# The first two pairs of a fused scan-and-MLP kernel: other loads, another way to the products of a, another order

## The chip, the cores and the metric

The kernel runs on one core of one Trainium2 chip. The core has TensorE (PE, matrix products into PSUM; the profile shows its weight loads apart, as PEld), VectorE (DVE), ScalarE (ACT) and GpSimd (POOL), each with its own queue of instructions that it works off in order. SyncE (SP) issues most of the transfers, ACT a few; sixteen DMA engines carry them. The metric is the device time of one execution in microseconds, median of several runs.

## The reference

Four batches of eight heads, 768 tokens each. `x` has 32 values per token and head, `B` and `C` 16, `a` one decay between 0.85 and 0.95.

```python
log_a = np.log(np.clip(a, 1e-06, 1.0))
for c in range(nc):                      # chunks of the sequence
    cum = np.cumsum(la, axis=-1)
    L = np.exp(cum[..., :, None] - cum[..., None, :]) * causal
    CB = np.einsum('bhin,bhjn->bhij', Cc, Bc)
    y_intra = np.einsum('bhij,bhjd->bhid', CB * L, xc)
    y_inter = np.einsum('bhin,bhnd->bhid', Cc, state) * np.exp(cum)[..., None]
    y[:, :, sl] = y_intra + y_inter
    state = decay_full[..., None, None] * state + np.sum(Bx, axis=2)
# then, with y as tokens (3072 x 256):
h = x @ w_in                             # 256 x 2048
g = np.maximum(h, 0.0) + alpha * np.minimum(h, 0.0)
out = g @ w_out                          # 2048 x 256
```

The weights `w_in` and `w_out` arrive as 64-bit floats, all else as 32-bit.

## The kernel before

The sequence is cut into chunks of 128 tokens; two chunks are a pair, so there are twelve pairs, three to a batch. Two pairs make a group of 512 tokens. For each pair the kernel makes, for eight heads, the matrix of decays by running products (a scan on VectorE, with ones of the identity as restarts), the Gram products of C and B on TensorE, multiplies both, adds the state's part and writes the transposed tokens `xT`. Then the MLP of that group runs: hidden products, the two-sided slope (`s_alpha` on ACT, `s_mul` on VectorE), output products. Groups 1 to 5 use a scheme with seven products instead of eight; group 0 is done plainly.

The order of each engine's work is that of the program text: a manual schedule, with waits added where one instruction needs another. So an instruction that waits holds all behind it on its engine.

**Weights.** Sixteen pieces of 512 KB, of 256 columns of `w_in` or two blocks of `w_out`, are loaded in turn (`load_next`, L257) into six buffers and turned to 32-bit in parts: `convert_a` takes the size of the high word on ACT (L273), clamps it on GpSimd, or on VectorE for piece 0 (L278), and takes the low half on ACT (L283, L286); `convert_b` moves it into place on VectorE (L308) with the sign of L296; `convert` adds both parts on GpSimd (L330).

**The first two pairs** are written out in `first_two`. They work on half chunks of 64 tokens, so that their decays come from one scan a bank (L871). Their steps:

- Loads of `load_pair`: `a` of pair 0 and of pair 1, broadcast to the 16 rows of each head (`load_a`, L133), B and C by token with 64 B runs (L192), x with 128 B runs (L197), the row form of `a` (96 rows for two batches, L126), alpha (L207). For pair 0, C, the row form and alpha are issued by ACT, all else by SP. The loads of pair 1 follow two weight pieces and two small stores (L500, L477).
- `first_a` clamps `a` (L437) into `z0` and `z1`; `spread` (L865) lays a head's row over the tokens by matmul; `scan` makes the decays.
- The running products of `a` that the states need: for pair 0 a scan over the broadcast row (L1000), for pair 1 a scan over the row form (`rows_short`, L497), stored to DRAM as `short` and read back as a broadcast (`load_second`, L231).
- B and C are turned by TensorE against the identity and copied by ACT (`turned`, L843, L847); C is parted by even and odd heads on ACT (`spread_c`, L854).
- `bn` is B times the decays from each token (L533); `added` (L895) makes the state's increments, `states` (L906, L910) the states, `mask` (L916) their masked forms.
- `gram_of` (L881), `times` (L887), `x_products` (L929), `state_products` (L941), `copy_out` (L949).
- `keep_warm` (L338) issues products of ones that nobody reads.
- Alpha is turned (L992), copied (L994), and `slopes` makes the tables of it.
- `hidden_two` (L1110) makes hidden blocks f and f+1 of one half of group 0. Blocks 0 and 1 of the first half run between the two pairs. Of blocks 2 and 3 the eight matmuls are woven into pair 1's steps by the function `among`.
- For pair 2 on, `rows_clamp`, `rows_out` and `rows_products` store the clamped rows (`z`, L477) and the running products (`pf`, L447), which come back as broadcasts (`abc`, L160; `ap`, L168).

After `first_two` come `hidden_two` of the second half (L1110), then `hidden` (L1095) and `output` (L1142) of group 0, with pairs 2 and 3 between, and from about 78 us the seven-product scheme (L1241, L1216).

## Time and profile before

| what | value |
|---|---|
| runs, us | 355.75, 355.75, 356.41; median 355.75 |
| span of the profiled execution, us | 355.9 |
| busy, us and share of the span | PE 349.3 (98%), PEld 284.4 (80%), DVE 235.8 (66%), ACT 171.8 (48%), POOL 204.4 (57%) |
| moved by DMA | 30.24 MB in 105581 packets, 79896 of them under 512 B |
| share of the DMA engines, first twelve slices of 8.9 us, tenths | 7 8 9 9 9 8 9 6 0 7 3 4 |
| DMA of SP's queue, 0 to 60 us | 34030 packets, 13.51 MB, 87.7% of 16 engines |

The profile was taken of one execution, and its times are of that execution alone. A row of a timeline reads: start, length, engine, line, operation, what is written and read, count, and in brackets the idle time of the engine before it and what ended that. A row of the chain of waits reads: start, length, engine and line; it follows back from the last instruction what each step waited for. SPq and ACTq rows are issues of transfers. A wait that came from several engines is put down to one of them. A busy TensorE is not one at its peak, as matmuls overlap.

### The profile page before, as it was taken

The page shows a single profiled execution, that of the slowest core. Times are in us where ns is not written, and L with a number is a line of the kernel's source. Part 1 is how long each engine was busy: PE and PEld are TensorE (multiplying, and loading weights), DVE is VectorE, ACT ScalarE, POOL GpSimd, SP SyncE. Part 2 cuts the span into 40 slices and gives each one's busy share as a digit, 9 for nine tenths or more (in the row PEclk, how much of TensorE's full clock was granted, in tenths as well). Part 3 has the DMA queues.
Part 4 walks back from the last instruction along what each step waited for, and adds up shares of the span by engine and source line. Part 5 has one row for each costly group of instructions (what it writes and reads, how often), then busy time and mean ns, then how long its engine had stood idle before and what let it go on. Part 6 is the DMA issues. An engine that isn't in the chain of part 4 may idle for free.

```text
span 355.9 us, 7778 instructions
## 1 busy us (share of the span) xinstructions
PE 349.3 (98%) x2985; PEld 284.4 (80%) x2985; DVE 235.8 (66%) x482; ACT 171.8 (48%) x391; POOL 204.4 (57%) x228
## 2 busy tenths in 40 slices
PE   8899999999999999999999999999999999999996
PEld 4576665578788888888888888888888888888885
DVE  6876986998748756847747856757856633643363
ACT  3477576535355346345345445345445344443431
POOL 6776568589939855725646626637526535434520
PEclk9999999999999999999999999999999999999999
DMA  7899989607345403503423423422001001001102
GB/s 138 182 202 270 329 174 279 148 17 159 106 83 128 102 3 75 104 2 77 78 57 74 86 51 71 85 55 65 11 2 31 0 2 29 2 1 31 31 0 59
DMA packets 105581, 30.24 MB, mean 85 GB/s; under 512 B 79896, under 2 KB 101448, under 8 KB 105544
## 3 DMA queue, kind: packets, MB, share of 16 engines
q1 hardware_dynamic: 103048, 29.43, 36.3%
q10 hardware_dynamic: 2496, 0.32, 0.6%
q8 instruction: 23, 0.38, 0.5%
q14 instruction: 14, 0.11, 0.1%
HBM read 26.32 MB, written 3.42 MB: 84 GB/s over the span
## 4 chain that ended last, share of the span: by engine, by line
PE 89%; SPq 4%; DMA 3%; DVE 2%; ACT 1%; POOL 1%; issue 0%; DVEq 0%; ACTq 0%
PE bank L1216 33%; PE hp L1241 29%; PE bank L1142 6%; PE ss L1241 6%; PE hp L1095 3%; DMA raw<-in_moe_w_in_dram 2%; SPq L192 2%; PE ss L787 1%; PE ss L731 1%; PE hp L1110 1%; PE bank L1209 1%; PE ss L805 1%; PE ss L779 1%; DMA xt<-in_x_dram 1%; SPq L197 1%; PE ss L742 1%
## 5 line engine op out<-in xcount | busy, mean ns | idle before, releaser
L1298 POOL TENSOR_TENSOR gt<-gt 128x512 f32<-128x512 f32 x58 | 74.2, 1279 | 21.1 <-DVE gt L1226 16.3
L1216 PE MATMUL bank<-gt,w_out 128*128 128x256 f32 x320 | 83.5, 381 | 0.0
L1216 PEld LDWEIGHTS bank<-gt,w_out 128*128 128x128 f32 x320 | 60.1, 190 | 9.2 <-issue 1.0
L1288 POOL TENSOR_TENSOR gt<-gt 128x512 f32<-128x512 f32 x20 | 25.4, 1269 | 62.5 <-DVE gt L1226 49.7
L1226 DVE SCALAR_TENSOR_TENSOR gt<-hp,s_mul,gt 128x256 f32<-128x256 f32 x96 | 42.0, 479 | 29.1 <-ACT gt L1224 26.8
L1224 ACT ACTIVATE gt<-hp,s_alpha 128x256 f32<-128x256 f32 x96 | 40.3, 471 | 34.5 <-PE hp L1241 31.4
L1216 PE MATMUL bank<-gt,ws 128*128 128x256 f32 x224 | 55.9, 379 | 0.0
L1216 PEld LDWEIGHTS bank<-gt,ws 128*128 128x128 f32 x224 | 42.3, 190 | 5.6
L1241 PE MATMUL hp<-xs,w_in 128*128 128x256 f32 x160 | 41.9, 384 | 0.0
L1241 PE MATMUL hp<-xs,ws 128*128 128x256 f32 x160 | 41.1, 380 | 0.0
L1267 DVE TENSOR_TENSOR hp<-hp,u 128x512 f32<-128x512 f32 x20 | 14.0, 700 | 35.2 <-ACT u L1265 35.2
L1241 PEld LDWEIGHTS hp<-xs,ws 128*128 128x128 f32 x160 | 30.3, 190 | 4.3 <-POOL xs L1183 0.2
L1241 PEld LDWEIGHTS hp<-xs,w_in 128*128 128x128 f32 x160 | 29.7, 190 | 4.5
L1142 PE MATMUL bank<-w_out,gt 128*128 128x256 f32 x128 | 31.1, 385 | 0.4 <-POOL w_out L330 0.4
L1142 PEld LDWEIGHTS bank<-w_out,gt 128*128 128x128 f32 x128 | 23.6, 190 | 7.2 <-issue 2.9
L1241 PE MATMUL ss<-xT,w_in 128*128 128x256 f32 x96 | 24.6, 379 | 0.0
L645 POOL TENSOR_TENSOR sm<-state,bmask 128x256 f32<-128x256 f32 (+1 forms) x10 | 6.2, 620 | 29.0 <-DVE state L642 29.0
L1095 PE MATMUL hp<-xT,w_in 128*128 128x512 f32 x48 | 22.8, 596 | 0.0
L561 DVE TENSOR_TENSOR_SCAN dec<-abc,bank 128x192 f32<-128x192 f32 x48 | 22.7, 522 | 0.0
L1256 ACT COPY m<-hp 128x512 f32<-128x512 f32 x8 | 4.7, 586 | 35.7 <-PE hp L1241 35.7
L1265 ACT COPY u<-hp 128x512 f32<-128x512 f32 x20 | 11.7, 585 | 19.4 <-PE hp L1241 19.4
L1226 DVE SCALAR_TENSOR_TENSOR gt<-c,s_mul,gt 128x256 f32<-128x256 f32 x40 | 20.6, 555 | 0.0
(232 smaller groups left out, 608.2 us busy)
## 6 DMA issues: line engine op xcount, KB each, us to landing
abc<-z SPq DMA_DIRECT2D x24, 192.0 KB
raw<-in_moe_w_in_dram SPq DMA_DIRECT2D x8, 512.0 KB
raw<-in_moe_w_out_dram SPq DMA_DIRECT2D x8, 512.0 KB
abc<-z SPq DMA_DIRECT2D x8, 512.0 KB
out_dram<-o_sb SPq DMA_DIRECT2D x32, 64.0 KB
nat<-in_B_dram SPq DMA_DIRECT2D x26, 64.0 KB
xt<-in_x_dram SPq DMA_DIRECT2D x12, 128.0 KB
xt<-in_x_dram SPq DMA_DIRECT2D x24, 64.0 KB
```

Of the source, the lines that this page charges most:

```text
L192: eng.dma_start(out=nat[:, i, k].rearrange("p (h n) -> p h n", h=H), in_=src[b, :, ts, :].rearrange("h p n -> p h n"))
L561: nc.vector.tensor_tensor_scan(out=dv[:, o : o + SQ], data0=abc[k][:, s : s + SQ], data1=ident_p[0][:, :SQ], initial=0.0, op0=ALU.mult, op ...
L1095: nc.tensor.matmul(hp, w_in[:, k, f * P : (f + 1) * P], xts[g][:, k], start=(k == 0), stop=(k == KC - 1))
L1142: nc.tensor.matmul(pos[0][t // 2][:, t % 2], gt[:, t * Q : (t + 1) * Q], w_out[:, f], start=(f == 0 and t % 2 == 0), stop=(f == NF - 1), s ...
L1216: nc.tensor.matmul(ms[g][i][:, h], w, blocks[g, z][n][:, p], start=(q == 0 and h == 0), stop=(q == NQ - 1), skip_group_check=True)
L1224: nc.scalar.mul(o[:, p], h[:, p], s_alpha[:, fs[p]])
L1226: nc.vector.scalar_tensor_tensor(out=o[:, p], in0=h[:, p], scalar=s_mul[:, fs[p]], in1=o[:, p], op0=ALU.mult, op1=ALU.max)
L1241: nc.tensor.matmul(to[:, p], w(2 * z + p), b, start=start and p == 0, stop=True, skip_group_check=True)
L1265: nc.scalar.copy(out=u2, in_=A)
L1267: nc.vector.tensor_tensor(out=Y, in0=Y, in1=u2, op=ALU.add)
L1288: nc.gpsimd.tensor_tensor(out=tc_, in0=g22, in1=g12, op=ALU.subtract)
L1298: eng.tensor_tensor(out=o, in0=x0, in1=x1, op=ALU.subtract)
```

## The change

The diff touches the loads of pairs 0 and 1, `first_two`, and small parts that these use.

- **a.** Pair 0's `a` is read with another stride, one run of 1 KB for each of 128 partitions, of which one per head holds the head's row. Pair 1's has one partition per head (8 runs), in a tile that VectorE clears first.
- **Products of a.** `short` is neither stored nor read back, and the scan of pair 0 goes. Both pairs' products come from the row form: a table `heads` of ones picks the row of each head by matmul (`products`), and ACT copies the results.
- **C.** C of both pairs comes in runs of 512 B (`load_blocks`, as pairs 5 on have it), and VectorE turns it (`turn_c`) straight into its place. B alone is turned by TensorE.
- **Order of loads.** SP: a, C, a of pair 1, x, weight piece 0, alpha, all of pair 1, piece 1. ACT: rows, B of pair 0. The stores of `z` and `pf` stand behind pair 1's work.
- **Engines and order.** Clamping pair 1's `a` goes to GpSimd. Piece 0 is converted by halves (`convert_first`), with the copies of pair 0's result in the middle. Piece 1's clamp goes to VectorE, and its conversion stands behind the scans of pair 1. Blocks 2 and 3 of the first half follow pair 1's products in one piece. Some of the `keep_warm` products get shorter, one goes, two come.

```diff
-    WARM = 2
-    def load_a(t, b, c, eng=nc.sync):
-        first = a[b, 0:1, c * Q : (c + 2) * Q]
-        eng.dma_start(out=t, in_=bass.AP(tensor=first.tensor, offset=first.offset,
-                                             ap=[[S, H], [0, N], [1, 2 * Q]]))
+    def load_a(t, c, spread=False):
+        first = a[0, 0:1, c * Q : (c + 2) * Q]
+        if spread:
+            nc.sync.dma_start(out=t, in_=bass.AP(tensor=first.tensor, offset=first.offset,
+                                                 ap=[[S // N, P], [1, 2 * Q]]))
+        else:
+            nc.sync.dma_start(out=t.rearrange("(h n) t -> h n t", n=N)[:, 0],
+                              in_=a[0, :, c * Q : (c + 2) * Q])
+    def load_blocks(nat, i, src, b, c):
+        for e in range(2):
+            first = src[b, e : e + 1, c * Q : (c + 2) * Q, :]
+            nc.sync.dma_start(out=nat[:, 1 + e, i],
+                              in_=bass.AP(tensor=first.tensor, offset=first.offset,
+                                          ap=[[2 * S * N, P // 32], [8 * N, 32], [1, 8 * N]]))
+    def turn_c(nat, to):
+        nc.vector.transpose(to.rearrange("p (c b) -> p b c", b=8),
+                            nat[:, 1:3, 1].rearrange("p e (b n) -> p b e n", n=N))
...
         def load_bc(k):
-            for i, src in enumerate((B,) if turned else (B, C)):
-                eng = nc.scalar if gp == 0 and i else nc.sync
+            eng = nc.scalar if gp == 0 else nc.sync
+            if gp == 0 and k == 0:
+                load_blocks(nat, 1, C, b, c)
+            for i, src in enumerate((B,) if turned or gp < NB else (B, C)):
...
+            if gp == 1 and k:
+                load_blocks(nat, 1, C, b, c)
...
+            if gp == 0 and k:
+                load_a(loads["a", 1], 2)
...
+    def convert_first(dst, src, sg, copies):
...
+        magnitude(0)
+        low(0)
+        magnitude(1)
+        nc.vector.tensor_single_scalar(out=r, in_=hi, scalar=SIGN, op=ALU.bitwise_and)
+        for k in range(2):
...
+        copies()
+        low(1)
+        for k in range(2):
+            nc.gpsimd.tensor_tensor(out=d[:, k], in0=r[:, k], in1=g.bitcast(U32)[:, k], op=ALU.add)
...
-    keep_warm(ps_h.tile([P, GT], F32, name="hp"), WARM, GT)
+    first = ps_h.tile([P, GT], F32, name="hp")
+    keep_warm(first, 1, GT)
+    keep_warm(first, 1, Q)
...
         if i == 0:
             scratch["z", 0] = dr.tile([RW, Q], F32, name="z0")
-            nc.sync.dma_start(out=scratch["z", 0], in_=held.pop("z"))
+            nc.gpsimd.memset(held[0][:, :1], 0.0)
+            nc.sync.dma_start(out=scratch["z", 0], in_=held[0][:, :Q])
...
+        def products(rpf, i, to):
+            for k in range(2):
+                nc.tensor.matmul(to[:, k * Q : (k + 1) * Q], heads[:, 2 * i + k], rpf,
+                                 start=True, stop=True, skip_group_check=True)
...
+        spread(z0, sp)
+        clamp(nc.vector, rq[:, :Q], rows)
+        clamp(nc.gpsimd, starts_r[:RW, ::HQ], rows[:, ::HQ])
+        masks_halved()
+        z1 = first_a(loads["a", 1], nc.gpsimd, lent[1][:, 2:])
+        heads = prep.tile([RW, 4, P], F32, name="heads")
...
+        turn_c(nat0, ct0)
+        prq, rpf = rows_short(rq)
         for r in range(4):
             scan(0, r, sp[r])
...
+        turn_b(nat0, hp)
+        copy_b(bc0, hp[:, : 2 * Q])
         bn0 = pair_loads(0)
+        for i in range(2):
+            products(rpf, i, pfs[:, 2 * i * Q : 2 * (i + 1) * Q])
+        nc.scalar.copy(out=pf0, in_=pfs[:, : 2 * Q])
+        cd0 = decayed_c(bc0, pf0)
+        nc.tensor.transpose(misc[:, Q : Q + NF], al_n, ident[:NF, :NF])
+        nc.scalar.copy(out=alpha, in_=misc[:, Q : Q + NF])
         gram_of(bc0, cz0, sp)
...
-        keep_warm(sp[0], 1, GT)
+        keep_warm(sp[0], 1, Q)
+        spread(z1, sp)
...
+        convert_first(*pieces[0], lambda: copy_out(0, y))
+        convert_next(first=False, ready=moe_w_in.dtype != F32)
+        keep_warm(sp[0][:, 2 * Q :], 1)
+        turn_c(nat1, ct1)
+        for r in range(4):
             scan(1, r, sp[r])
...
+        prelu_of = {0: hidden_two(0, 0, 0, first)}
         bn1 = pair_loads(1)
...
         added(dps, bn1, xt1)
+        gram_of(bc1, cz1, sp)
+        keep_warm(own[1][:, : 2 * Q], 2)
         states(1, dps, pf1, range(3))
         one_at_a_time(1, range(3))
+        convert_a(*pieces[1], by=nc.vector)
+        prelu_of[0](False)
+        convert_b(*pieces[1])
+        convert_next(first=False)
+        for r in range(4):
+            times(1, r, sp[r])
+        states(1, dps, pf1, (3,))
+        y = places([own[0], bank(0)], [bank(1), bank(2)])
+        x_products(y, xt1, 1)
+        state_products(y, 1, cd1)
+        copy_out(1, y)
+        prelu_of[0]()
+        prelu_of[2] = hidden_two(0, 2, 0, second)
+        rows_clamp(0)
         rpf = rows_products()
         load_bc()
         load_next()
+        rows_out(0)
         rows_sent(rpf)
...
-    load_next(2)
+    load_next()
+    nc.sync.dma_start(out=al_n, in_=moe_alpha.rearrange("(k p) -> k p", p=P))
+    load_pair(1)
+    load_next()
```

## The prediction

> **What bounds the kernel now.** I read the share of each engine first, then TensorE's busy time by stretches, its waits, the chain of waits of the first 48 us, and last the single instructions of each queue there. The stretches (columns: stretch, its length, then busy time and count of PE, PEld, DVE, ACT, POOL; PEclk, DMA share, GB/s):
>
> ```profile
> 0.00:5.00 5.00, 4.17 (x21) 1.66 (x29) 2.97 (x13) 1.28 (x1) 3.66 (x16) 1.00 0.64 85
> ...
> 10.00:15.00 5.00, 4.15 (x106) 2.64 (x86) 4.60 (x14) 3.01 (x8) 2.84 (x5) 1.00 0.83 144
> 15.00:20.00 5.00, 4.75 (x83) 3.49 (x81) 3.44 (x7) 2.60 (x7) 4.80 (x8) 1.00 1.01 210
> ```
> ```profile
> 46.00:100.00 54.00, 54.00 (x432) 39.20 (x433) 43.83 (x75) 28.10 (x58) 41.03 (x41) 1.00 0.58 146
> 100.00:200.00 100.00, 100.00 (x823) 85.82 (x822) 67.11 (x136) 50.24 (x120) 58.76 (x61) 1.00 0.35 71
> ```
>
> From 46 us on TensorE never stops. Whatever the change does must show as an earlier or later start of that unbroken row; behind 46 us it edits nothing. Before 46 us, the only waits of TensorE from 18 us on are these:
>
> ```profile
> PE bank L1142 <- POOL w_out L330: 0.4, 1, 0.4
> PE bank L929 <- DVE dec L887: 0.3, 1, 0.3
> ```
>
> So from about 24 us TensorE runs dense, with one hole of 0.44 us at 45.4. The end is set by two runners: the front (pairs 0 and 1, done at about 24 us) and the weights that land behind it. The chain shows both:
>
> ```profile
> 14.22 3.28 DMA xt<-in_x_dram
> ...
> 23.28 2.35 PE hp L1110 x10
> 25.63 1.74 PE bank L1110 x8
> ...
> 29.84 7.45 DMA raw<-in_moe_w_in_dram
> ...
> 44.52 1.28 POOL w_out L330
> 45.84 1.99 PE bank L1142 x8
> ```
>
> The front waits until 17.5 for x of pair 1; the weight piece that lands at 37.3 leads, through conversions, to the hole.
>
> **The loads.** Prices: the B and C loads of 64 B runs moved 1126 packets in 0.50 us (23.75 to 24.25), so 1024 take 0.46 us; x at 128 B moved 1426 in 1.00 us, so a tile takes 0.72; weights at 2 KB moved 186 in 1.00 us, so a piece of 256 takes 1.4. C in 512 B runs has no row. Its bounds are 64 KB at the 364 GB/s of the weights, 0.18 us, and 0.46 (no gain); I take 0.22, nearer the larger runs. Four C blocks save 1.0 us. The a row of pair 1 shrinks from 128 packets to 8 and the broadcast of `short` goes: 128 KB each at 364 GB/s, 0.35 each. The store of `short` saves about 0.1. In all 1.8 us of transfer less (bounds 0.8 to 1.9), and SP no longer sits in issues like this one:
>
> ```profile
> 9.40 3.52 SPq L192 DMA_DIRECT2D nat<-in_B_dram  x1
> ```
>
> New order on SP: a, C, C, a of pair 1, x, x, weights 0, alpha, then B, B, C, C, x, x of pair 1, weights 1. Pair 1 passes weights 1 and two stores; the alpha row leaves ACT's queue for SP's, behind 512 KB. B of pair 0 moves to ACT's queue. Packets of pair 0 (96 rows of 512 B, 128 of 1 KB, 2048 of 64 B, 256 of 512 B, 2048 of 128 B) cost, by the prices above, about 3.3 us of full rate against 4.1 before. Before, they were through at about 7.0; so 6.2 after. Weights 0 then end at 7.6, alpha just behind. A transfer is usable later than its last packet: the alpha row's queue ran dry at 5.4, and its reader started at 6.66, 1.2 us later. So **alpha lands at 8.8**. Bounds: 7.4 (straight after x, if the small row overtakes), and 10.3, since weights 0 before were read at 11.54 though by rate they ended at 8.9, a lag of 2.65. I take the small row's own lag. Pair 1's x ends 0.9 + 0.4 + 1.4 after 7.6 and lands at 11.5, six us earlier than 17.5, and is no gate any more.
>
> **The alpha wait.** Alpha's transpose stands ahead of the Gram products on TensorE, and alpha's copy ahead of the first state on ACT. These rows show the steps of before:
>
> ```profile
> 6.66 0.14 PEld L992 LDWEIGHTS ss<-ident,al_n 16*128 16x128 f32 x1 [0.17 <-DMA al_n<-in_moe_alpha_dram]
> 8.27 0.73 PE L881 MATMUL bank<-cz,bc 32*64 32x128 f32 x32 [0.53 <-ACT alpha L994]
> 8.97 0.76 DVE L887 TENSOR_TENSOR dec<-bank,dec 128x256 f32<-128x256 f32 x2 [0.40 <-PE bank L881]
> ```
>
> Gram began at 8.27, VectorE's products 0.70 later. Now Gram begins 0.2 after alpha, at 9.0, and the products at 9.7. Without alpha the gate would be VectorE's scans: first scan 5.55 before; its queue gains a transpose of C (0.55, half of the 1.11 that line 574 takes for twice the elements) and par (0.17), loses memsets, and may start about 0.2 earlier, as the warming matmuls no longer hold the spread until 4.5. Scans end at 8.4 against 7.98. So alpha costs 1.3 us there; SP's loads behind it are not held, as SP does not wait.
>
> **VectorE from there.** Its steps before x products of pair 1, from their rows: products and states of pair 0, 8.97 to 11.34, 2.37; weights 0, sign 0.40, clamp 0.43, xor 0.76, 1.59; transpose of C, 0.55; four scans, 2.43; three states, 0.92; weights 1, sign, clamp (now VectorE's, was GpSimd's) and xor by start-to-start steps, 0.34 + 0.34 + 0.61 = 1.29; four products, 1.36. Sum 10.5; end at 20.2. Before they ended at 21.50: **1.3 us earlier**. The removed scan for the products of a (0.67) and the clamp of a (0.28, now GpSimd's) are already out of this sum; rows_products (0.83) and its GpSimd clamp (0.63) move behind it. The head products, four small matmuls, lie in TensorE's idle time before Gram; if that cover went they would cost about 0.4, four times the 0.1 step of a transpose.
>
> One stall can come in: weights 0 end in ACT's second low half, behind copy-out, then a GpSimd half (0.85), then bn of pair 1 (1.15), which TensorE needs for the states. Worked through, it delays states by 0 to 0.65; I take 0.1, since before bn1 ended at 16.89, which is where VectorE's scans end now (16.6).
>
> **What it gives back on TensorE.** Before, hidden 2 and 3 of the first half were woven among pair 1's products: when these ended at 23.28, two of eight matmuls remained, and the second half began near 23.9. Now all eight follow. Eight at 0.217 (25.63 to 27.37 for eight) are 1.74 against 0.61: **1.1 us lost**. Copy-out hides beneath it. So the dense row begins 1.3 - 0.1 - 1.1 = 0.1 earlier.
>
> **The hole.** GpSimd's clamp of rows, rows_products, z's store and pf's store now follow pair 1 on their queues: z is stored near 22.4 (it was 7.38), pf near 22.9 (24.15). SP stands there: x of pair 2, weights 5, the decay broadcasts and weights 6 wait behind. Weights 2 to 4 are issued ahead and land meanwhile. Before, weights 6 were issued at 29.84; now pf + 2 us to land, broadcast, 0.5 each for four issues: about 26. With 1.8 us less to move, weights 6 land 2 to 3 us before 37.3, and the 0.44 closes. If this cover failed, an earlier front would only lengthen the hole.
>
> Later small gains: VectorE gets weights earlier, and TensorE's steps of 1.81 and 1.83 instead of 1.72 around 31 to 35 may shrink: 0.2 (0 to 0.4). **Sum**: 0.1 + 0.44 + 0.2, about 0.8 us off. The span is 355.9; the median of the runs, 355.75, lies 0.15 below it. 355.75 - 0.8 = **354.9**.
>
> The Trainium skill, TensorE: Matmul & The Clock Gate, Part 1, speaks against the change: an array that has been idle for about 3.4 us runs at half clock until as long a busy stretch has passed. This trace bears on it: four matmuls of 512 columns take 3.75 us at the start, 0.94 each, and 1.72 at 25 us and later, 0.43 each, while the granted clock reads 1.00 in both. By the rule, warming cut to about 2.3 us might leave the array slow beyond 9 us; the sum would then be some 1.5 us longer. I leave it out of the forecast.
>
> **The rivals.**
> *Larger gain.* Alpha lands by 7.5, so scans gate at 8.4, and VectorE's row begins 1.1 us earlier: 353.8, with up to 0.6 more where start-to-start steps are shorter than I took: 353.3. For it: the row is 8 KB. Against: it stands behind 512 KB on each ring.
> *Slower by alpha.* Each us that alpha lands after 8.8 is one us on Gram, VectorE and the end. It breaks even at 9.6 and costs 0.2% from 10.3. With the 2.65 lag of weights 0 it lands at 10.3; with the full bn stall, 0.55 more, 354.9 + 1.5 + 0.55 = 357.0. For it: the row of 11.54. Against: those weights had 512 KB more behind them, now small packets follow.
> *Slower by the clock.* Half speed for Gram (0.73 more) and for the hidden matmuls after the waiting stretch of 18 to 20 us (up to 1.7): 354.9 + 1.5 = 356.4. For it: the trimmed warming; against: a burst of matmuls ahead of that stretch.
> *The weights pin it.* If weights 6 come no earlier, the hole swallows the front's gain: 355.75. Against: all rows above.
> *Not what it says:* C in 512 B runs saves nothing: 1.0 us of transfer back, which lands on alpha by half: 355.3.
>
> **How the numbers follow.** Forecast (353.9 to 355.7 as its own range) 0.44; larger gain 0.26; alpha late 0.13; clock 0.07; weights pin it, and no saving, 0.10. A run of this kernel can be told from no change by about 0.2%, that is outside 355.04 to 356.46. The forecast's 0.44 splits into 0.28 faster, 0.12 same and 0.04 slower, the clock's 0.07 into 0.02 same and 0.05 slower, the last 0.10 into 0.08 same and 0.02 slower. Faster: 0.28 + 0.26 = 0.54. Same: 0.12 + 0.02 + 0.08 = 0.22. Slower: 0.13 + 0.04 + 0.05 + 0.02 = 0.24. The range runs from the larger gain to the alpha case, 353.0 to 357.0.
>
> **What would show it.** Right: alpha's transpose on TensorE waits for its DMA until about 8.8, VectorE's products of pair 0 start near 9.7, those of pair 1 end near 20.2, x of pair 1 is waited for by nobody, the second half of hidden begins near 23.8, and no wait for weights stands at 45 us. Wrong: a Gram stage begun by 8.3; matmuls of 256 columns at 0.43 instead of 0.217 after 9 us; a TensorE wait for a weight piece between 24 and 46 us; scans of pair 1 after 17.5.

## The result, and the profile after

| | runs, us | median, us | profiled execution, span us |
|---|---|---|---|
| before | 355.75 355.75 356.41 356.80 356.20 | 356.20 | 355.9 |
| changed | 365.19 366.95 367.18 367.05 367.40 | 367.05 | 363.5 |

The changed kernel is slower: the ratio is 1.0297, with a 95% interval of 1.0274 to 1.0321. The forecast of 354.9 us with a range of 353.0 to 357.0 was wrong in size and in sign.

The stretches of the changed kernel show first that TensorE runs short of work (columns as before; the second number is PE busy, the number behind POOL's is the granted clock):

```profile
0.00:5.00 5.00, 3.63 (x36) 1.97 (x36) 1.94 (x11) 1.90 (x2) 2.93 (x14) 1.00 0.58 99
5.00:10.00 5.00, 2.71 (x11) 2.48 (x12) 3.70 (x8) 1.53 (x4) 1.70 (x2) 1.00 0.89 184
10.00:15.00 5.00, 4.71 (x134) 3.32 (x133) 2.92 (x10) 1.92 (x7) 2.72 (x7) 1.00 0.96 261
15.00:20.00 5.00, 4.50 (x67) 3.06 (x73) 4.28 (x8) 3.22 (x10) 2.66 (x6) 1.00 0.80 154
20.00:25.00 5.00, 2.15 (x72) 1.43 (x73) 3.17 (x9) 0.92 (x3) 2.28 (x5) 1.00 0.67 161
25.00:30.00 5.00, 4.99 (x84) 4.16 (x85) 2.53 (x8) 1.72 (x6) 2.14 (x4) 0.54 0.16 36
30.00:35.00 5.00, 5.00 (x20) 4.21 (x19) 2.88 (x7) 3.00 (x8) 3.84 (x6) 0.77 1.03 307
```

TensorE has two holes, at 5 to 10 us and at 20 to 25 us. Behind the second the granted clock falls to 0.54, and from 25 to 35 us TensorE is busy throughout and still slow. The 1.00 of the first rows is no measurement: the trace's list of granted clocks begins at 11.79 us, with the rise to full speed. The two longest waits of TensorE name both holes:

```profile
PE ss L970 <- DVE dec L928: 2.8, 1, 2.8
PE ss L1035 <- DVE gt L538: 2.1, 1, 2.1
```

VectorE's queue shows where its time went (L152 is the new transpose of C, L538 the scan of the row form, L928 the products of decays and Gram matrices, L912 the scans of pair 1, L951 the states, L385 a warming product):

```profile
5.78 0.64 DVE L152 STREAM_TRANSPOSE bc<-nat 128x256 f32<-128x256 f32 x1 [2.02 <-DMA nat<-in_C_dram]
6.48 0.42 DVE L538 TENSOR_TENSOR_SCAN gt<-rq,gt 96x128 f32<-96x128 f32 x1
...
11.95 0.76 DVE L928 TENSOR_TENSOR dec<-bank,dec 128x256 f32<-128x256 f32 x2 [2.40 <-PE bank L922]
...
17.69 2.43 DVE L912 TENSOR_TENSOR_SCAN dec<-bank,ident_q 128x256 f32<-128x256 f32 x4 [0.68 <-PE bank L385]
...
22.16 0.60 DVE L951 SCALAR_TENSOR_TENSOR gt<-gt,ap,ss 128x64 f32<-128x64 f32 x2 [1.40 <-PE ss L385]
...
24.50 1.41 DVE L928 TENSOR_TENSOR dec<-bank,dec 128x256 f32<-128x256 f32 x4
```

It idles 2.02 us for C, and the row scans, which had nothing to do with C, stand behind that wait. It idles 2.40 us for the Gram products, and twice (0.68 and 1.40) for a product that nobody reads. TensorE ahead of the Gram products (L896 are the head products, L1047 is alpha, L922 Gram, L936 the increments):

```profile
8.72 1.91 PE L896 MATMUL ss<-gt,heads 96*128 96x128 f32 x8
10.57 0.28 PE L1047 MATMUL ss<-ident,al_n 16*128 16x16 f32 x1
10.78 1.16 PE L922 MATMUL bank<-cz,bc 32*64 32x128 f32 x32
11.87 0.59 PE L936 MATMUL hp<-xt,bn 64*32 64x64 f32 x32
```

Alpha waited for nothing. The four head products are eight records and take 1.91 us, where the forecast had idle time, or 0.4. Up to the Gram products TensorE runs at half speed; the increments are the first at full speed. The chain of waits tells the rest of the story, from pair 1's warming to the end of the second half's hidden products:

```profile
21.06 1.08 PE ss L385 x4
22.16 0.29 DVE gt L951
22.48 0.28 DVE gt L951
22.76 0.50 DVE wr L343
23.26 0.61 DVE wt L325
23.93 0.57 issue
24.50 0.43 DVE dec L928
24.97 0.24 PE ss L970
...
28.52 5.52 PE hp L1154 x16
34.04 1.73 PE bank L1154 x8
```

While VectorE makes the states and converts weight piece 1 (L343, L325, and L355 inside the gap that reads "issue"), TensorE has nothing from 22.13 to 24.97. Then sixteen records of hidden products take 5.52 us, 0.345 each, where the eight behind them take 1.73, 0.216 each.

By milestones, from the timelines of both kernels. Two rows of before that the table needs, the last scans and the decay products of pair 1:

```profile
16.31 1.26 DVE L871 TENSOR_TENSOR_SCAN dec<-bank,ident_q 128x256 f32<-128x256 f32 x2
...
20.08 1.42 DVE L887 TENSOR_TENSOR dec<-bank,dec 128x256 f32<-128x256 f32 x4
```


| stretch | before, us | changed, us | difference |
|---|---|---|---|
| start to pair 0's first decay product | 8.97 | 11.95 | +2.98 |
| from there to the end of pair 1's scans | 8.60 | 8.17 | -0.43 |
| to the end of pair 1's decay products | 3.93 | 5.79 | +1.86 |
| to the end of its state products | 1.78 | 2.61 | +0.83 |
| to the end of the second half's hidden products of 256 columns | 4.09 | 7.25 | +3.16 |
| sum | 27.37 | 35.77 | +8.40 |

Behind that TensorE is dense in both, and the changed kernel has no wait for weights left. So +8.40 less the hole of 0.44 and some small gains gives the 7.6 between the two spans. The runs differ by 10.85. In every run of the study that lists both, the time is the span plus about 1.7 us; by that the profiled execution of before took 357.6, longer than any of the five listed, and that of the changed kernel, 365.19, is the shortest of its five. So the table sets a long execution beside a short one and leaves some 3.2 us out. A likely part of these is seen in e1, e2, e3 and e10 below: with the changed kernel's warming they first reach full speed at 19.0 to 23.0 us, where the profile shown here does at 11.8. The changed kernel's longer runs were not profiled, so this is not shown.

### The profile page after: what moved, and what is told of

It is laid out like the page before. It is cut to its first block, busy times and chain, and to the rows that moved or that the text cites. A ratio compares the mean times of both kernels' runs of the same rounds, so it can differ in the third digit from the quotient of the medians.

```text
span 363.5 us, 7792 instructions
## 1 busy us (share of the span) xinstructions
PE 352.7 (97%) x2989; PEld 289.5 (80%) x2989; DVE 238.8 (66%) x484; ACT 173.0 (48%) x394; POOL 202.9 (56%) x226
## 4 chain that ended last, share of the span: by engine, by line
PE 95%; DVE 2%; DMA 1%; issue 0%; SPq 0%; POOL 0%; ACT 0%; DVEq 0%; POOLq 0%
PE bank L1256 33%; PE hp L1281 28%; PE bank L1182 8%; PE hp L1139 6%; PE ss L1281 6%; PE hp L1154 2%; PE ss L830 1%; PE ss L774 1%; DMA nat<-in_C_dram 1%; PE bank L1249 1%; PE ss L848 1%; PE ss L822 1%; PE ss L785 1%; PE ss L661 1%; PE ss L385 1%; PE bank L922 0%
## 5 line engine op out<-in xcount | busy, mean ns | idle before, releaser
L1281 PEld LDWEIGHTS hp<-xs,w_in 128*128 128x128 f32 x160 | 29.7, 190 | 4.5
```

The lines of the kernel that those rows point to most:

```text
L1281: nc.tensor.matmul(to[:, p], w(2 * z + p), b, start=start and p == 0, stop=True, skip_group_check=True)
```

## The experiments

The line numbers in an experiment's rows are those of its own kernel and can differ by one to four from the changed kernel's. Ratios are against the kernel before.

**e1: a filled hole.** Warming products in the gap ahead of pair 1's x products.

```diff
         states(1, dps, pf1, (3,))
+        keep_warm(second, 3, GT)
         y = places([own[0], bank(0)], [bank(1), bank(2)])
```

> The changed kernel with three more warming products of 512 columns on TensorE, written to a bank nobody reads, in its idle stretch of 22.1 to 25.0 us. Clock theory (the idle stretch halves TensorE's clock from 25.3 to 32.2 us): granted clock 1.00 all through, x products of pair 1 to the end of hidden 0 to 3 in 8.1 us instead of 10.8, total 2.5 to 3.5 us less (about 363.5 against 367). Rival (the clock is a bystander, VectorE and the weights set the pace behind 25 us): clock 1.00 and total within 0.7 us of 367.

365.49 us (362.58 to 366.09), ratio 1.0223 (1.0175 to 1.0271). The timeline of VectorE:

```profile
19.59 2.44 DVE L912 TENSOR_TENSOR_SCAN dec<-bank,ident_q 128x256 f32<-128x256 f32 x4 [1.82 <-PE bank L385]
...
25.46 0.60 DVE L951 SCALAR_TENSOR_TENSOR gt<-gt,ap,ss 128x64 f32<-128x64 f32 x2 [1.40 <-PE ss L385]
```

The clock is held: the granted clock reads 1.00 from 20 to 50 us. But only some 1.6 us come back. In the profiled execution the warming waits ahead of pair 1 were longer (1.82 instead of 0.68), and the profile has a wait for weights again (0.26). The longer waits are not the edit's doing: up to there the program is that of the changed kernel, but this execution stayed at half speed up to 23.0 us. The first hidden products, first in the changed kernel's profile, then in e1's:

```profile
17.81 2.17 PE L1154 MATMUL hp<-xT,w_in 128*128 128x256 f32 x8
```
```profile
19.77 3.51 PE L1155 MATMUL hp<-xT,w_in 128*128 128x256 f32 x8
```

So the late clock loss is a consequence of the gap, and not all of the loss; and half speed in the front lasts longer in some executions of one program than in others.

**e2: rows first.** The row scans ahead of the transpose of C on VectorE, the copy of the row products ahead of C's parting on ScalarE.

```diff
-        turn_c(nat0, ct0)
         prq, rpf = rows_short(rq)
+        turn_c(nat0, ct0)
```

> The changed kernel with the two scans of the row form ahead of the transpose of C on VectorE, and the copy of the turned row products ahead of the first spread of C on ACT. Theory that the wait for C (VectorE idle to 5.78 us) holds the front through the queue order: the row scans end near 5 instead of 7.2, the head products begin before 8, the first products of pair 0 on VectorE begin near 10.5 instead of 11.95, total 1.2 to 2 us less. Rival (the Gram stage is held by the head products at half clock or by C itself): they begin after 11.5, total within 0.6 us.

366.37 us (365.48 to 367.25), ratio 1.0274 (1.0249 to 1.0299). Alpha's transpose on TensorE:

```profile
9.15 0.28 PE L1047 MATMUL ss<-ident,al_n 16*128 16x16 f32 x1 [0.74 <-DMA al_n<-in_moe_alpha_dram]
```

With C's wait out of the row scans' way, alpha becomes the gate that the forecast named, at 9.15 instead of 8.8. Pair 0's decay products start at 10.53 instead of 11.95, 1.4 us earlier. Pair 1's scans then wait 1.82 us for the warming product in their bank, in an execution that reaches full speed only at 19.0 us. So the start moved as expected and the time did not: the median is 0.7 us less, and the interval overlaps that of the changed kernel.

**e3: warming elsewhere.** The warming behind pair 1's Gram products goes to a bank that nobody waits for.

```diff
-        keep_warm(own[1][:, : 2 * Q], 2)
+        keep_warm(second[:, 2 * Q :], 2)
```

> The changed kernel with the two warming products after the Gram stage of pair 1 written to the bank of the turned B instead of the bank that holds the states' increments. Bank theory (VectorE's second and third state wait for these products): VectorE's states end near 21.4 instead of 22.8, its products of pair 1 end near 24.5 instead of 25.9, TensorE's idle stretch shrinks to about 1.4 us, the clock stays at 1.00, total 4 to 5 us less. If the stretch alone does not set the clock: 1.4 us less and the clock drops as before. Rival (the states wait for the increments themselves): nothing moves.

364.83 us (364.37 to 365.47), ratio 1.0232 (1.0214 to 1.0251). The 1.40 is gone: VectorE makes the three states in one row, 0.98 us, from 22.29. TensorE's idle ahead of the x products falls to 1.58, the clock falls for 3.4 us instead of 6.8 (0.73 from 25 to 30 us instead of 0.54), and the sixteen hidden records take 4.86 instead of 5.59 in the timeline.

**e4: the price of not weaving.** The kernel before, with hidden blocks 2 and 3 behind pair 1's products in one piece.

```diff
-        prelu_of[2] = hidden_two(0, 2, 0, second, among)
+        y = places([own[0], bank(0)], [bank(1), bank(2)])
+        x_products(y, xt1, 1)
+        state_products(y, 1, cd1)
+        copy_out(1, y)
+        prelu_of[2] = hidden_two(0, 2, 0, second)
```

> The kernel before with one part of the change alone: the eight matmuls of hidden blocks 2 and 3 of the first half follow pair 1's products in one piece instead of being woven among them. Theory from the forecast: 1.1 us more than before less what the idle time it leaves gives back, so 0.6 to 1.3 us more. Rival (TensorE's idle stretch that this leaves lets the clock fall): 3 us more or above, with a granted clock below 1.00 near 23 us.

357.12 us (356.69 to 360.32), ratio 1.0034 (1.0012 to 1.0056), 0.9 us against the forecast's 1.1 (the interval is 0.4 to 2.0). Its sixteen hidden records take 3.72 us: the full-speed size of the changed kernel's 5.59.

**e5 and e6: the warming, alone and with the rows.** e5 gives the changed kernel the warming lengths of before (two of 512 columns at the start, 384 behind the row transposes, 512 ahead of the second spread); e6 adds the edit of e2.

```diff
-    keep_warm(first, 1, GT)
-    keep_warm(first, 1, Q)
+    keep_warm(first, 2, GT)
...
-        keep_warm(misc[:, Q:], 1, Q)
+        keep_warm(misc[:, Q:], 1, 3 * Q)
...
-        keep_warm(sp[0], 1, Q)
+        keep_warm(sp[0], 1, GT)
```

> The changed kernel with the warming products as long as before at three places: two of 512 columns at the start, 384 columns after the turned row products, 512 ahead of the spread of pair 1's a. Theory that the shortened warming keeps TensorE at half speed through the front: the head products take 0.9 us instead of 1.9, Gram of pair 0 0.73 instead of 1.16, first hidden eight 1.9 from the start, state products of pair 1 end 2 to 3 us earlier (near 26), total 2 to 4 us less, the later drop of the clock staying. Rival (VectorE's queue alone sets the front, TensorE's speed is hidden): the matmuls are faster, the end of the state products and the total stay within 0.7 us.

> As the warm start, and the row scans ahead of the transpose of C as well. If the wait for C and the half clock are both costs of the front they add: pair 0's first products on VectorE near 9.5 to 10, total 1 to 1.5 us below the warm start alone. Rival (only one of them gates): no change against the warm start.

e5: 369.85 us (366.81 to 370.63), ratio 1.0391 (1.0367 to 1.0416). e6: 365.13 us (362.52 to 367.30), ratio 1.0245 (1.0176 to 1.0314). Alone, the longer warming is a loss: TensorE still idles 2.01 us for the row scans behind C, the head products still take 1.92, and 1.65 us of warming now stand in their way. e6 falls into two groups, 362.5 and 363.0 against 367.3 twice; its profile is of the 362.52 us execution. There, with the rows first, two rows of TensorE show a front at full speed and a middle that is not:

```profile
7.20 1.06 PE L895 MATMUL ss<-gt,heads 96*128 96x128 f32 x8
...
25.87 5.51 PE L1153 MATMUL hp<-xT,w_in 128*128 128x256 f32 x16
```

The head products' full-speed size is 1.06 us. The longest idle of TensorE in this execution, 19.56 to 22.40, is followed by half speed again.

**e7 and e8: the middle's waits taken away.** Both are e6 without the warming in the scans' bank. e7 puts the other one just behind the Gram products into a spare bank, three times 512 columns; e8 puts two of 256 there and converts piece 1 ahead of the states.

```diff
-        keep_warm(sp[0][:, 2 * Q :], 1)
...
-        keep_warm(own[1][:, : 2 * Q], 2)
+        keep_warm(second[:, 2 * Q :], 2)
+        convert_a(*pieces[1], by=nc.vector)
+        convert_b(*pieces[1])
         states(1, dps, pf1, range(3))
         one_at_a_time(1, range(3))
-        convert_a(*pieces[1], by=nc.vector)
         prelu_of[0](False)
-        convert_b(*pieces[1])
```

> As the last, and the warming products in the banks of the increments and of the scans are gone; three of 512 columns go to the bank of the turned B after the Gram stage of pair 1, in TensorE's idle stretch. Bank and clock theories together: scans of pair 1 and the states start without a wait for warming, clock 1.00 from 20 to 35 us, hidden 0 to 3 of both halves in 5.2 us, total 4 to 6 us below the warm start with rows, so about 357 to 359. Rival (weights hold the row then): a wait of TensorE for a weight piece of 1 us or more appears after 30 us.

> As the last, with the conversion of weight piece 1 on VectorE ahead of the states instead of between states and products of pair 1, and two warming products of 256 columns instead of three of 512. Theory that this conversion lies on the path: products of pair 1 end 1 us earlier than in the last and the total is 0.5 to 1.5 us less. Rival (the states wait for the increments no longer than the conversion takes): no difference.

e7: 359.88 us (359.29 to 362.91), ratio 1.0118 (1.0072 to 1.0164). e8: 360.25 us (359.86 to 360.96), ratio 1.0114 (1.0095 to 1.0132). Some 5 us come back with either, by medians; against the shorter two runs of e6 it is 2.5 to 3. Converting piece 1 ahead of the states (e8) shows no gain over e7. The profiled execution of e7 is its longest, 362.91, and has its own lesson, in a stretch:

```profile
10.00:15.00 5.00, 4.83 (x121) 2.33 (x109) 4.65 (x13) 1.47 (x5) 2.72 (x7) 0.57 0.87 211
```

TensorE had waited 1.80 us for alpha, until 9.32; the granted clock is 0.57 from 10 to 15 us, 0.50 from 15 to 20, and VectorE then waits 4.45 us for pair 1's increments.

**e9 and e15: the trimmed warming by itself.** The kernel before, with only its warming cut to the changed kernel's lengths. e15 is the same kernel once more, for a second profile.

```diff
-    keep_warm(ps_h.tile([P, GT], F32, name="hp"), WARM, GT)
+    first = ps_h.tile([P, GT], F32, name="hp")
+    keep_warm(first, 1, GT)
+    keep_warm(first, 1, Q)
...
-        keep_warm(al_p[:, Q:], 1, 3 * Q)
+        keep_warm(al_p[:, Q:], 1, Q)
...
-        keep_warm(sp[0], 1, GT)
+        keep_warm(sp[0], 1, Q)
```

> The kernel before with one thing changed: its warming products cut to the sizes the changed kernel has (512+128 columns at the start instead of 2x512, 128 instead of 384 behind the row transposes, 128 instead of 512 ahead of the second spread). If the shorter warming alone costs what the changed kernel lost, this runs 3 us or more longer (above 359) and its products of the front stand at half speed: a spread of 32 products takes 1.16 to 1.28 us instead of 0.69. If the warming was longer than needed, the time stays within 0.7 us of before (355.6 to 357.0) and the spread stays at about 0.7 us; then the loss is in the new order of the front and middle, not in the trimming.

> The kernel of e9 once more, for a profile of an execution with the longer time: seven of its ten executions took 358.1 to 360.1 us and three 356.5, the profiled one among the three. If the 3 us are TensorE's clock, a profile of a 359 us execution shows matmuls at half speed (spread of pair 1 1.16 instead of 0.69, hidden products of 256 columns 0.41 instead of 0.27) over some 3 to 7 us in the first 30 us, that the profile of the 356.5 us execution does not have. If it is something else, the first 30 us are alike and the difference lies further on.

e9: 359.33 us (356.48 to 360.12), ratio 1.0062 (1.0031 to 1.0093). Its ten runs fall into two groups: 356.48, 356.51, 356.53, and seven from 358.05 to 360.12. The profile of e9 is of the 356.51 us execution, that of e15 of one of 359.30. The same rows of TensorE, first e9:

```profile
9.05 0.73 PE L883 MATMUL bank<-cz,bc 32*64 32x128 f32 x32 [0.74 <-ACT alpha L996]
...
13.34 0.69 PE L867 MATMUL bank<-gt,ident 32*64 32x128 f32 x32
14.43 1.99 PE L1112 MATMUL hp<-xT,w_in 128*128 128x256 f32 x8 [0.40 <-POOL w_in L330]
```

and e15:

```profile
9.05 1.19 PE L883 MATMUL bank<-cz,bc 32*64 32x128 f32 x32 [0.60 <-ACT alpha L996]
...
14.88 1.16 PE L867 MATMUL bank<-gt,ident 32*64 32x128 f32 x32
15.96 3.39 PE L1112 MATMUL hp<-xT,w_in 128*128 128x256 f32 x8
```

Up to 9.05 us the two executions agree, both at half speed (their first spread takes 1.16 us); e9 is at full speed from there, e15 only from about 19 us, and the second half's hidden products start at 28.08 instead of 25.29: 2.8 us, the difference of the two times. The granted clock reads 1.00 in every stretch of both, but the trace's list of it begins at 8.02 us in e9 and at 18.82 in e15, against 5.24 in before. So the trimming does not make the clock fall; it puts off its first rise, which alone costs 2.8 us in most executions and little in some (of the kernel before, one run of thirteen beside e9 was that long, 358.87). The rival that the warming was longer than needed holds for three of ten.

**e10: C ahead of B.** The changed kernel with pair 0's B issued by SP behind C, and alpha by ScalarE right behind the rows.

```diff
-            eng = nc.scalar if gp == 0 else nc.sync
+            eng = nc.sync
...
             load_rows(0, nc.scalar)
+            nc.scalar.dma_start(out=al_n, in_=moe_alpha.rearrange("(k p) -> k p", p=P))
```

> The changed kernel with pair 0's B issued by SyncE behind C, and alpha by ScalarE right behind the rows of a. If B's 64 B packets on ScalarE's queue held C back, the transpose of C starts at 5.0 us or earlier (5.78 in the changed kernel), the row scans end by 6.4 (7.22), and the alpha transpose waits for no DMA; the time falls by no more than 1.5 us (365.5 to 367), because the hole ahead of pair 1's x products and the half-speed stretch behind it stay. If C is late for reasons of its own, the transpose still starts at 5.6 or later. B's transposes then start later than 8 us if B is the next thing late.

366.82 us (366.28 to 367.20), ratio 1.0296 (1.0277 to 1.0315): no difference from the changed kernel. C's transpose starts at 5.37 and still waits 1.74 us for C. In the nine profiles with the changed kernel's order of loads it starts at 5.78 to 6.67, in the five with this one at 5.26 to 5.55. So taking B away from beside C is worth 0.2 to 1.4 us of its lateness; the rest stays open.

**e11 and e12: weaving again.** On e8, hidden blocks 2 and 3 go among pair 1's products: x products, half of the hidden, state products and their copy, the other half. e12 is that alone; e11 has the loads of e10 too.

```diff
-        state_products(y, 1, cd1)
-        copy_out(1, y)
-        prelu_of[0]()
-        prelu_of[2] = hidden_two(0, 2, 0, second)
+
+        def among(k):
+            if k == 0:
+                state_products(y, 1, cd1)
+                copy_out(1, y)
+                prelu_of[0]()
+
+        prelu_of[2] = hidden_two(0, 2, 0, second, among)
```

> e8 (longer warming, rows first, warming out of the increments' and scans' banks, piece 1 converted ahead of the states) with the loads of e10, and with hidden blocks 2 and 3 of the first half woven into pair 1's products again: x products, half of the hidden, state products, the other half. If low use of TensorE during the x and state products, after the idle stretch, is what lowers the clock at 23.6 us in e8, the granted clock stays above 0.95 from 20 to 35 us, 16 hidden products of the second half take 3.5 to 4.0 us, and the time is 355.5 to 358.0. If the idle 0.9 us ahead of the x products alone does it, the clock falls again to about 0.8 and the time stays at 359 to 361.

> e11 without the loads of e10 (B on ScalarE ahead, alpha on SyncE behind): the weaving alone on e8. Weaving is worth 1.5 to 3 us against e8 (357.2 to 358.8) if the clock is held; the difference to e11 is what C's and alpha's landing cost: 0.5 to 1.5 us if the front is on the path, none if the front's gain is swallowed by waits on TensorE as it was when the rows alone were moved.

e11: 359.37 us (358.43 to 360.38), ratio 1.0079 (1.0052 to 1.0106). e12: 360.94 us (359.64 to 362.57), ratio 1.0134 (1.0099 to 1.0169). In both the granted clock stays at 1.00 from 20 to 35 us, where e8 had 0.86 and 0.80 from 20 to 30, although TensorE still idles 0.9 us ahead of the x products. e12's time doesn't follow: it is not below e8's, so weaving alone gives nothing that these runs can tell, and the 1.5 to 3 us expected of it were wrong. The profiles show where it goes: the hidden products of 256 columns end at 29.6 to 29.7 us instead of 30.8, but TensorE then waits 1.0 us for a piece of `w_out`, and the output products start at 33.06 (e11: 32.98) where e8 has 32.94. e11 is below e8 by 0.9 and below e12 by 1.6, with intervals that overlap, so the loads' share is not settled.

**e13, e14 and e16: the front and the middle.** e13 is e11 with pair 1's head products behind pair 0's Gram products and no warming behind the row transposes.

```diff
-        for i in range(2):
-            products(rpf, i, pfs[:, 2 * i * Q : 2 * (i + 1) * Q])
+        products(rpf, 0, pfs[:, : 2 * Q])
...
         gram_of(bc0, cz0, sp)
+        products(rpf, 1, pfs[:, 2 * Q :])
...
-        keep_warm(misc[:, Q:], 1, 3 * Q)
```

> e11 with the front's TensorE work cut down to what the Gram matrices of pair 0 wait for: pair 1's head products go behind those Gram matrices, and the warming behind the row transposes (two records, 1.65 us in e11) is left out. If the rest of e11's loss (3.2 us) is this chain (warming 1.65, head products of pair 1 0.95), the Gram matrices start at 8.0 to 9.0 us (10.20 in e11), the first hidden block 1.2 to 2.2 us earlier than 16.18, and the time is 357.0 to 358.2. If the front's TensorE then falls to half speed for longer, or waits on TensorE further on swallow it as they did when the rows alone were moved, the time stays within 0.6 us of e11 (358.8 to 360.0).

361.40 us, four runs: 359.02, 359.92, 362.88, 362.89; ratio 1.0163 (1.0117 to 1.0208). In the profiled 359.02 us execution Gram starts at 7.42, where before it was 8.27, and the first hidden block at 14.80 (16.18 in e11). TensorE loses part of it at the wait that e11 and e12 have too:

```profile
31.60 1.99 PE L1186 MATMUL bank<-w_out,gt 128*128 128x256 f32 x8 [1.03 <-POOL w_out L378]
```

The longer two runs were not profiled. e14 adds an order of the middle in which piece 1's last VectorE step stands behind pair 1's decay products, its clamp goes back to GpSimd, and piece 2 begins ahead of the x products.

```diff
-        convert_a(*pieces[1], by=nc.vector)
-        convert_b(*pieces[1])
+        convert_a(*pieces[1])
+        sign(*pieces[1])
         states(1, dps, pf1, range(3))
...
             times(1, r, sp[r])
+        convert_b(*pieces[1])
+        convert_next(first=False)
         states(1, dps, pf1, (3,))
+        convert_a(*pieces[2])
+        sign(*pieces[2])
```

> e13 with VectorE's and ScalarE's order in the middle changed: the clamp of piece 1 goes back to GpSimd, its last VectorE step behind the four times of pair 1, and the first steps of piece 2 ahead of pair 1's products, as the kernel before has them. It should take away the 0.9 us ahead of the x products (x products start 1.0 to 1.9 us earlier than in e13) and the 1.02 us that TensorE waits for w_out at 33 us. Theory: another 1 to 2 us, 355.2 to 357.2, level with before. Rival: hidden blocks 2 and 3 then wait for piece 1 (VectorE's last step and GpSimd's addition come later by about 1.5 us), the idle moves behind the x products and the time is that of e13 within 0.6 us.

364.57 us (362.68 to 366.36), ratio 1.0237 (1.0196 to 1.0278). The rival holds, and more than it said; TensorE:

```profile
27.01 1.13 PE L1158 MATMUL hp<-xT,w_in 128*128 128x256 f32 x4 [1.82 <-POOL w_in L378]
...
29.97 5.26 PE L1158 MATMUL hp<-xT,w_in 128*128 128x256 f32 x12
```

Hidden blocks 2 and 3 wait 1.82 us for piece 1, and the twelve records behind them run at half speed: 0.44 each. Its profiled execution, the longest of its four, has another half-speed stretch in the front (granted clock 0.50 from 10 to 20 us). e16 is e13 with piece 2 begun early, as in e14, but piece 1 left where it was, and with warming where TensorE idled behind pair 0's increments and pair 1's Gram products.

```diff
         added(dps, bn0, xt0)
+        keep_warm(misc[:, 2 * Q :], 2)
...
-        keep_warm(second[:, 2 * Q :], 2)
+        keep_warm(second[:, 2 * Q :], 3)
...
         states(1, dps, pf1, (3,))
+        convert_a(*pieces[2])
+        sign(*pieces[2])
```

> e13 with two more warming records behind pair 0's increments and one more behind pair 1's Gram matrices, and with the first steps of piece 2 (ScalarE's magnitudes, GpSimd's clamp, VectorE's signs) ahead of pair 1's products, as the kernel before has them. Theory: the wait of 1.03 us for w_out at 31.6 us goes, and fewer executions fall into the longer half-speed stretch (two of e13's four were at 362.9, two at 359.0 and 359.9): 357.0 to 358.5 with a spread under 2 us. It is not expected to beat the kernel before, whose second half's hidden products start 0.9 us earlier than in e13's shorter executions. Rival: the longer and the shorter executions stay as they are (359 and 363), and the clock isn't ruled by these two idle places.

358.59 us (357.73 to 359.44), ratio 1.0070 (1.0054 to 1.0087). Both expected signs are there: the runs lie within 1.7 us instead of 3.9, and output products start without a wait, at 30.41. Of the 10.85 us lost, 8.5 are back; no version tried beats the kernel before. In the profile of e16 the output products start 0.95 us later than in that of before (29.46). What makes up the rest of the 2.4 us in its other executions stays open.

## Why the prediction was wrong

**The step that failed first: the front.** The forecast gave pair 0's decay products 9.7 and alpha as the gate; they started at 11.95, and alpha waited for nothing. Two terms were wrong. The text gave the transpose of C its 0.55 on VectorE and no wait. It worked out when alpha and x land, but not when C does: C was read at 5.78, after 2.02 us of idle, and the program puts the row scans behind it. And the head products, four small matmuls that the text put into TensorE's idle time, at about 0.4 if that cover went, are eight records, 1.06 us at full speed (e6) and 1.91 as they ran, in line ahead of alpha and Gram, because the row scans that feed them came late: the cover was gone. e2 shows that the alpha step itself was sound: with the rows first, alpha is the gate at 9.15, and 9.18 and 9.32 in e6 and e7, 0.35 to 0.5 behind the 8.8 of the text. Of the 2.25 us that pair 0's products came late, e2's profile takes 1.42 away; of the 0.83 left there, 0.37 is the start of Gram (9.37 for 9.0) and 0.45 its half speed (1.18 for 0.73).

**The step that cost most: the middle.** The sum for VectorE, 10.5 us from pair 0's products to the end of pair 1's, added durations as if nothing on TensorE could hold VectorE there. It took 13.96. Of the 3.46 more, 1.40 and 0.68 are waits for warming products that the diff puts into the banks of pair 1's increments and scans, and 0.37 the wait for the increments; the rest is longer steps, above all the two exclusive-ors of piece 0 (0.42 and 0.91 for 0.76 in all) and the three steps of piece 1 (1.82 from start to start for 1.29). The text called the new warming a help to the clock and never asked who reads the bank that it writes. e3 took the 1.40 alone and gave 2.2 us.

**The same step, its other half.** The text moved piece 1's conversion into VectorE's sum and did not ask what TensorE does meanwhile. It idled 2.85 us there. Nothing else was ready for it: hidden blocks 2 and 3, which are woven into pair 1's steps in the kernel before, now follow pair 1's products, and they read piece 1, which VectorE was only then converting. Moving both took the cover away. The price of the unweaving alone was right: 0.9 in e4.

**The clock rival was right in kind and less than half the size.** It had a chance of 0.07 and a price of 1.5 us, and was left out of the sum. By rows of this case half speed cost 5.59 - 3.72 = 1.9 us on the sixteen hidden records, about 0.8 on pair 1's products, and 0.85 on the head products, and the trimming by itself 2.8 us in most executions of e9. The Trainium skill, TensorE: Matmul & The Clock Gate, Part 1, which the text cited against the change, puts the idle that slows the array at about 3.4 us. Here 2.85 us were enough in the changed kernel and 1.58 in e3; the measurement decides. The same Part (What's actually happening) adds that the window runs freely, so that one kernel has more or fewer slow products from run to run. e9 and e15, one kernel with 2.8 us between two executions, agree.

**What was right.** Nobody waits for pair 1's x any more; scans, states and products have the sizes of their rows.

**What came true by luck.** The hole of 0.44 at 45 us closed, but not because weights came earlier. z's store came at 27.59 instead of 22.4, as its work came late, and weights 6 were issued at 31.76, where the text had 26 and before 29.84. The piece that TensorE had waited for was ready at 53.22 instead of 45.79, 7.4 us later; TensorE's row was 8.4 us late and reached it at 53.37. Nor did SP stop sitting in issues: one of x, at 13.11, took 4.05 us.

**The base.** The span of the profiled execution was set beside the median as if it were its time. With the 1.7 us around it, it was 1.85 above that median, longer than any run listed. The hole may belong to that execution alone: e9, a kernel with the loads of before, has none in its execution of 356.51 us. The row that waited until 45.84 in before starts here at 44.78, and TensorE is busy throughout (columns of the stretches):

```profile
40.00:50.00 10.00, 10.00 (x106) 6.40 (x106) 9.44 (x17) 6.11 (x11) 5.27 (x6) 1.00 0.95 218
```

So the 0.44 in the sum, more than half of its gain, may never have been there to win in an ordinary run. And the three terms make 0.74, not 0.8: 355.0.

**What is shown, and what is argued.** Shown by removal: the wait on the increments' bank (e3), the trimmed warming on the kernel before (e9, e15), the unwoven blocks (e4). For the order of rows and C, e2 shows the earlier start but no time that can be told apart; e6 against e5 is 4.7 us by medians, with e6 in two groups. e7 and e8 show that the middle's waits together are worth 2.5 to 5 us on top of e6. That the fall of the clock follows from the idle ahead of the x products is shown by e1, where filling it held the clock. The idle is not all of it: e8 and e11 both idle 0.90 us there, and the clock fell in e8, where only the products in small pieces follow, and held in e11, where full hidden products stand among them. Not settled: most of C's late landing, when the front first reaches full speed in an execution, the longer executions of e6 and e13, and the last 2.4 us.

## What to carry to other kernels

Before moving work off an engine that seems to have slack, list for every new wait what stands behind it in that queue, and for every product that only keeps the array busy, who next reads its bank. An array kept at speed by filler is part of the schedule: an edit that shortens the filler or opens one to three microseconds of idle is priced at the slow speed of everything that follows, here for 3 to 14 us. And several small holes in series hide each other, so that taking away one gives little (e2, e10) where taking away all gives back most (e16).

## What the hardware showed

- Every profile begins at half speed, and the granted clock does not show it: the rows before the first rise read 1.00 because nothing is recorded there. A spread takes 1.16 us instead of 0.69 (416 ns a record instead of 268). The length of a known product is the surer sign, record by record: the 1.28 us of the changed kernel's second spread hold two waits, and its records take 268 ns.
- By the traces' lists of granted clocks the first rise comes at 3.9 to 13.3 us in the eleven profiles with the longer warming, and at 8.0 to 23.0 in the seven with the trimmed one. A later fall is recorded (0.50 in e7, in e14 and behind the middle's gap), and every recorded stretch of 0.50 before the kernel's end lasts 3.41 us or a multiple of it.
- The fall came late: TensorE ran dry at 22.13, and the granted clock fell at about 25.5, with work running again since 24.97. It came back between 32 and 33, some 4 us into the dense hidden products that began at 28.52; the products in pieces of 64 rows before them had not brought it back.
- Idle well under 3 us was enough: 1.58 us in e3, 1.80 us for alpha in the profiled execution of e7, and 0.90 in e8, though not in e11 and e12.
- Transfers of 64 B packets on ScalarE's queue ran beside C's 512 B packets on SP's: with both at once, 169 packets moved on SP's queue from 2.5 to 4.25 us and 1939 on the other. Taking B out of the way brought C 0.2 to 1.4 us earlier (e10 and the four after it with its loads).
